# Split weights written to memory by the first batch and loaded finished by the other three

## The chip, the cores and the metric

The kernel runs on one core of a Trainium2 chip. The metric is device time in microseconds (us). The time before is 846.46 us, the median of three runs (843.69 to 851.68). The profiled execution is one more run of the same program, 848.2 us, with a span of 845.7 us from its first to its last instruction.

## The reference

Inputs arrive in float64, the attention's q, k and v in float32. B is 4, S is 448, the width is 768 (12 heads of 64). What is computed, for each batch:

```python
scores = q @ k.T / sqrt(64); mask above the diagonal; attn = softmax(scores)
x      = (attn @ v)                      # heads side by side: 448 x 768
gate   = sigmoid(causal_conv5(x, conv_w))
h      = gate * (x @ w_val)              # weight stage 0
x2     = h @ w_out                       # weight stage 1
theta  = x2 @ w_theta                    # weight stage 2
y      = w_tok_r @ (x2 * cos(theta)) + w_tok_i @ (x2 * sin(theta))
u      = x2 + y
out    = u + relu(u @ w_ch)              # weight stage 3
```

Four of the weights (w_val, w_out, w_theta, w_ch) are 768 x 768 and serve all four batches alike.

## The kernel before, in words

Every large matmul is made of three: a float32 operand x is split into a high part (rounded to the engine's fp32r format) and a low part (x minus high), and high*high, high*low and low*high are summed in PSUM. So each weight has to become a pair (high, low) in SBUF before TensorE (PE) can use it.

A weight stage has 6 column blocks of 128, and the four stages make 24 blocks, numbered n = 0 to 23 in batch 0, 24 to 47 in batch 1, and so on to 95 (`NW * B` = 96). A block is cut into two halves (g = 0, 1) of 384 rows; a half is a tile of 128 partitions x 384 elements. Half a block feeds 9 matmuls of 448 columns (`gemm`, L452).

A half goes through three steps:

- `load_w` (batch 0 only): a DMA of 384 KB brings the 64-bit words into a `cv_raw` buffer (3 KB a partition, 4 buffers).
- `stage_w`: in batch 0 `to_f32` turns the 64-bit words into float32 with three VectorE (DVE) operations (L152, L155, L159) and one of ScalarE (ACT, L158); the last one writes the `w_raw` tile (1.5 KB, 3 buffers), which a DMA (L210) also writes to a scratch tensor in memory. In the later batches a DMA (L212) loads `w_raw` from the scratch tensor.
- `split_w`: GpSimd (POOL) makes the high part (`pool_hi`, L104), and POOL (`pool_lo`, L107) or DVE (`dve_lo`, L110) the low part, into `w_hi` and `w_lo` (1.5 KB, 3 buffers each). It runs in all four batches. `W_DVE` says per batch and stage how many of the two halves' low parts go to DVE.

`gemm(n)` calls, for each half, `split_w` of block n+1, `stage_w` of block n+2 and `load_w` of block n+4, and then issues its 9 matmuls. The first two blocks (`AHEAD` = 2) are split into tiles of the activations' buffers and used by `gemm_ahead` while batch 0's attention runs.

Around it: all DMAs are issued from one queue, that of SyncE (SP), in order; an instruction on it that waits holds all behind it. Besides the weights these are q, k and v of the next heads, the results, and for each pair of heads the row sums' reciprocals, which go to memory (`rows<-rec`, L375) and come back spread over partitions (`rb<-rows`, L378). The dense stages of batch b run while the attention of batch b+1 is computed; the table `RATE` says how many attention steps stand between the dense steps. The framework's scheduler puts each engine's instructions in an order that is fixed before the run, and hands out the buffers of a tag.

Of the kernel before, what the change touches and what calls it, by code (L numbers as in the profile page):

```python
# [37 lines left out]
YLD = 1  # L38
ABS_DVE = (1, 0, 0, 0)
PIN = 2  # L40
W_DVE = ('0010', '1000', '0000', '2111')
TOK_AFTER = 5
LAG = 3
RATE = ((1.027, 1.063, 1.027), (1.029, 1.029, 1.089), (1.03, 1.03, 1.01), (1.057, 0.994, 1.041))
# [4 lines left out]
def kernel(  # L49
# [86 lines left out]
            )  # L136

    def setup_conv():
        t = pool.tile([P, CV, 2], I32, tag="cv_raw", name="cv_raw", bufs=4)
# [42 lines left out]
        dve_lo(wtok_l[:, m, :], pt[:, :S], wtok_h[:, m, :])  # L182

    stages = [w_val, w_out, w_theta, w_ch]
    scratch = dram.tile([NW, 2, P, KH * P], F32, name="scratch")
    bits = {}
    raws = {}
    splits = {}

    def load_w(n, g):  # L190
        if n < NW:
            e = n % KC
            t = pool.tile([P, CV, 2], I32, tag="cv_raw", name="cv_raw", bufs=4)
            nc.sync.dma_start(
                out=t.rearrange("p (c n) two -> p c (n two)", c=KH),
                in_=stages[n // KC][g * KH * P : (g + 1) * KH * P, 2 * e * P : 2 * (e + 1) * P].rearrange(
                    "(c p) n -> p c n", p=P
                ),
            )
            bits[n, g] = t  # L200

    def stage_w(n, g):
        if n >= NW * B:
            return
        t = pool.tile([P, KH, P], F32, tag="w_raw", name="w_raw", bufs=3)
        flat = t.rearrange("p c n -> p (c n)")
        if n < NW:
            to_f32(flat, bits.pop((n, g)))
            if B > 1:
                nc.sync.dma_start(out=scratch[n, g], in_=flat)  # L210
        else:
            nc.sync.dma_start(out=flat, in_=scratch[n % NW, g])  # L212
        raws[n, g] = t

    def split_w(n, g):
        if n >= NW * B:
            return
        t = raws.pop((n, g))
        if n < AHEAD:
            hi, lo = (  # L220
                pool.tile([P, S], F32R, tag=tag, name="w_ahead", bufs=12)[:, : KH * P].rearrange("p (c n) -> p c n", n=P)
                for tag in ("act_hi", "act_lo")
            )
        else:
            hi = pool.tile([P, KH, P], F32R, tag="w_hi", name="w_hi", bufs=3)
            lo = pool.tile([P, KH, P], F32R, tag="w_lo", name="w_lo", bufs=3)
# [213 lines left out]
    def gemm(acts):  # L440
        n = wn[0]
        wn[0] += 1
        pt = psum("mm")
        for g in range(2):
            split_w(n + 1, g)
            stage_w(n + 2, g)
            load_w(n + 4, g)
            whi, wlo = splits.pop((n, g))
            for kc in range(g * KH, (g + 1) * KH):
                xhi, xlo = acts[kc]  # L450
                for m, (a, x) in enumerate(((whi, xhi), (whi, xlo), (wlo, xhi))):
# [187 lines left out]
    for n in range(5 * (H + 1) + X_SEG + 1):  # L639
        next(at, None)  # L640
        if n == 5:
            setup_conv()
        for m in range(AHEAD):
            if n == W_AT + 4 * m:
                for g in range(2):
                    load_w(m, g)
            if n == W_AT + 4 * m + 2:
                for g in range(2):
                    stage_w(m, g)
                    split_w(m, g)  # L650
        i, c = divmod(n, 5)
        if AHEAD and i >= 4 and i % 2 == 0 and c == A_SEG and i // 2 - 2 < KC - 1:
            gemm_ahead(i // 2 - 2)
        if n == 5 * H - 5:
            for m in range(AHEAD, AHEAD + 2):
                for g in range(2):
                    load_w(m, g)
            for g in range(2):
                stage_w(AHEAD, g)
                load_w(AHEAD + 2, g)  # L660
        if n == 5 * H:
            for g in range(2):
# [52 lines left out]
```

## Time and profile before

| | before |
|---|---|
| median of three runs | 846.46 us (843.69 to 851.68) |
| profiled execution | 848.2 us, span 845.7 us |
| PE busy | 732.9 us (87%) |
| POOL busy | 515.9 us (61%) |
| DVE busy | 521.2 us (62%) |
| ACT busy | 414.1 us (49%) |
| mean granted clock of PE | 0.938 |
| moved by DMA | 88.28 MB |

The share of an engine is its busy time over the span. A granted clock of 1.00 is 2.4 GHz, of 0.5 is 1.2 GHz. The difference between the execution's time and its span, 2.5 us, lies outside the profile.

### The profile page before, as it was taken

The page shows a single profiled execution, that of the slowest core. Times are in us where ns is not written, and L with a number is a line of the kernel's source. Part 1 is how long each engine was busy: PE and PEld are TensorE (multiplying, and loading weights), DVE is VectorE, ACT ScalarE, POOL GpSimd, SP SyncE. Part 2 cuts the span into 40 slices and gives each one's busy share as a digit, 9 for nine tenths or more (in the row PEclk, how much of TensorE's full clock was granted, in tenths as well). Part 3 has the DMA queues.
Part 4 walks back from the last instruction along what each step waited for, and adds up shares of the span by engine and source line. Part 5 has one row for each costly group of instructions (what it writes and reads, how often), then busy time and mean ns, then how long its engine had stood idle before and what let it go on. Part 6 is the DMA issues. An engine that isn't in the chain of part 4 may idle for free.

```text
span 845.7 us, 12489 instructions
## 1 busy us (share of the span) xinstructions
PE 732.9 (87%) x3965; PEld 611.6 (72%) x3965; DVE 521.2 (62%) x1161; ACT 414.1 (49%) x982; POOL 515.9 (61%) x589
## 2 busy tenths in 40 slices
PE   6577589888397896999889898989989999999997
PEld 4446358666296785878768786868778787898996
DVE  6775698979878562744747644725637834436641
ACT  6667465545567642435558632525558621125311
POOL 3566559667434656577768745567848348676322
PEclk9879669999599898999989999999989999999999
DMA  9984743768534343444423224345332113433113
GB/s 223 185 146 85 139 89 106 206 174 176 181 91 107 61 119 102 82 125 100 101 57 82 52 69 108 89 118 98 84 92 49 32 49 103 132 112 84 36 31 102
DMA packets 151277, 88.28 MB, mean 104 GB/s; under 512 B 93455, under 2 KB 150317, under 8 KB 151213
## 3 DMA queue, kind: packets, MB, share of 16 engines
q1 hardware_dynamic: 151213, 87.51, 42.8%
q8 instruction: 31, 0.51, 0.3%
q14 instruction: 33, 0.27, 0.1%
HBM read 72.45 MB, written 15.03 MB: 103 GB/s over the span
## 4 chain that ended last, share of the span: by engine, by line
PE 47%; DMA 21%; DVE 18%; issue 4%; ACT 4%; POOL 3%; SPq 2%; ACTq 0%; POOLq 0%; DVEq 0%
PE ps_mm L452 23%; PE ps_mm L545 10%; DMA rows<-rec 7%; PE ps_av L357 4%; DMA w_raw<-scratch 4%; PE ps_tr L334 3%; DMA cv_raw<-in_moe_w_val_dram 3%; DMA cv_raw<-in_moe_w_ch_dram 2%; PE ps_s L313 2%; DMA cv_raw<-in_moe_w_theta_dram 2%; DVE w_raw L159 2%; DVE ps_s L315 2%; PE ps_s L314 2%; DVE gate L415 2%; PE ps_tr L531 1%
## 5 line engine op out<-in xcount | busy, mean ns | idle before, releaser
L104 POOL TENSOR_SCALAR w_hi<-w_raw 128x384 fp32r<-128x384 f32 x188 | 113.6, 605 | 151.1 <-PE ps_mm L452 90.1
L452 PE MATMUL ps_mm<-act_hi,w_lo 128*128 128x448 f32 x432 | 163.0, 378 | 8.3 <-POOL w_lo L107 6.4
L452 PE MATMUL ps_mm<-act_hi,w_hi 128*128 128x448 f32 x432 | 163.6, 381 | 6.5 <-POOL w_hi L104 2.1
L107 POOL TENSOR_TENSOR w_lo<-w_raw,w_hi 128x384 fp32r<-128x384 f32 x146 | 157.2, 1078 | 9.3
L452 PE MATMUL ps_mm<-act_lo,w_hi 128*128 128x448 f32 x432 | 159.9, 370 | 0.0
L115 ACT ACTIVATE prob<-ps_s,negm 112x112 f32<-112x112 f32 x192 | 95.2, 497 | 88.3 <-DVE negm L315 86.4
L315 DVE CUSTOM_DVE_ANT_0 ps_s<-ps_s,mask 112x112 f32<-112x112 f32 x192 | 85.6, 454 | 65.1 <-PE ps_s L314 54.4
L334 PE MATMUL ps_tr<-ident,prob 112*112 112x112 f32 x480 | 85.2, 280 | 19.0 <-ACT prob L115 13.1
L452 PEld LDWEIGHTS ps_mm<-act_hi,w_lo 128*128 128x128 f32 x432 | 82.9, 192 | 19.4 <-POOL w_lo L107 10.1
L452 PEld LDWEIGHTS ps_mm<-act_hi,w_hi 128*128 128x128 f32 x432 | 82.4, 192 | 16.0 <-POOL w_hi L104 4.0
L313 PE MATMUL ps_s<-kk,qs 128*112 128x256 f32 x192 | 74.0, 389 | 20.2 <-ACT prob L115 10.3
L452 PEld LDWEIGHTS ps_mm<-act_lo,w_hi 128*128 128x128 f32 x432 | 82.9, 192 | 5.5
L334 PEld LDWEIGHTS ps_tr<-ident,prob 112*112 112x112 f32 x480 | 59.3, 142 | 34.2 <-ACT prob L115 17.9
L107 POOL TENSOR_TENSOR act_lo<-x2f,act_hi 128x448 fp32r<-128x448 f32 x36 | 44.9, 1247 | 53.9 <-DVE act_hi L464 28.4
L347 ACT COPY pt<-ps_tr 112x448 f32<-112x448 f32 (+2 forms) x120 | 51.4, 441 | 48.3 <-PE ps_tr L334 47.6
L357 PE MATMUL ps_av<-pt,v_raw 112*64 112x336 f32 (+3 forms) x384 | 66.4, 451 | 1.7 <-ACT pt L347 1.3
L314 PE MATMUL ps_s<-klo,qs 128*112 128x256 f32 x192 | 62.8, 339 | 3.3 <-DVE klo L110 3.1
L545 PE MATMUL ps_mm<-wtok_h,zt_h 128*128 128x448 f32 x168 | 64.4, 383 | 0.5 <-ACT zt_h L536 0.4
L545 PE MATMUL ps_mm<-wtok_h,zt_l 128*128 128x448 f32 x168 | 63.6, 379 | 1.4 <-DVE zt_l L110 1.3
L545 PE MATMUL ps_mm<-wtok_l,zt_h 128*128 128x448 f32 x168 | 62.0, 369 | 0.0
L411 POOL TENSOR_TENSOR gate<-gate,tp 128x448 f32<-128x448 f32 x48 | 58.8, 1225 | 2.4
L313 PEld LDWEIGHTS ps_s<-kk,qs 128*112 128x112 f32 x192 | 36.7, 192 | 29.1 <-ACT prob L115 12.3
(101 smaller groups left out, 1518.3 us busy)
## 6 DMA issues: line engine op xcount, KB each, us to landing
w_raw<-scratch SPq DMA_DIRECT2D x144, 192.0 KB, 2.4
scratch<-w_raw SPq DMA_DIRECT2D x48, 192.0 KB, 2.8
q_raw<-in_q_dram SPq DMA_DIRECT2D x48, 112.0 KB, 3.0
k_raw<-in_k_dram SPq DMA_DIRECT2D x48, 112.0 KB, 3.3
v_raw<-in_v_dram SPq DMA_DIRECT2D x24, 224.0 KB, 3.2
rb<-rows SPq DMA_DIRECT2D x48, 112.0 KB, 3.3
out_dram<-o SPq DMA_DIRECT2D x24, 224.0 KB, 2.7
cv_raw<-in_moe_w_val_dram SPq DMA_DIRECT2D x12, 384.0 KB, 4.7
```

Of the source, the lines that this page charges most:

```text
L104: nc.gpsimd.tensor_scalar(out=dst, in0=src, scalar1=1.0, scalar2=0.0, op0=ALU.mult, op1=ALU.add)
L107: nc.gpsimd.tensor_tensor(out=dst, in0=src, in1=f32(hi), op=ALU.subtract)
L115: exps.append(nc.scalar.activation(*args, **kw))
L313: nc.tensor.matmul(pt[:CP, :nn], lhsT=qs[:, cs], rhs=kk[:, :nn], start=True, stop=False)
L314: nc.tensor.matmul(pt[:CP, :nn], lhsT=qs[:, cs], rhs=klo[:, :nn], start=False, stop=True)
L315: ttr = nc.vector.tensor_tensor_reduce(out=pt[:CP, :n], in0=pt[:CP, :n], in1=mask[:, S - n : S], scale=-1.0 / math.sqrt(D), scalar=3.0e38, ...
L334: nc.tensor.transpose(pt[:CP, off : off + CP], prob[i, c][:, kc * CP : (kc + 1) * CP], ident[:CP, :CP])
L347: nc.scalar.copy(t, src)
L357: nc.tensor.matmul(av[g][j * D : (j + 1) * D, kc * CP : S], lhsT=tv[:, j, kc, :], rhs=pT.pop((2 * g + j, kc)), start=kc == 0, stop=kc == N ...
L411: nc.gpsimd.tensor_tensor(out=gt, in0=gt, in1=tp, op=ALU.add)
L452: nc.tensor.matmul(pt[:, :S], lhsT=a[:, kc % KH, :], rhs=x, start=kc == 0 and m == 0, stop=kc == KC - 1 and m == 2,)
L545: nc.tensor.matmul(pt[:, :S], lhsT=a[:, m, :], rhs=w[:, m, :], start=m == 0 and n == 0, stop=m == NZ - 1 and n == 2,)
```

## The change

Only batch 0 stages and splits. `stage_w` writes the float32 words back into every second word of the `cv_raw` tile itself (so `w_raw` is gone), `split_w` reads them from there with a step of two words, and both parts go to memory: one DMA of 384 KB from the joint tile `w_hl` (high and low side by side, 3 KB), or for the first two blocks two DMAs of 192 KB. In the other three batches a new function, `fetch_w`, loads the finished pair with one DMA of 384 KB into a `w_hl` tile; `gemm(n)` calls it for block n+3. `load_w` moves from block n+4 to n+3. `cv_raw` and `w_hl` share one tag, `wb`, of 8 buffers of 3 KB, in place of the 4 buffers of 3 KB and 9 of 1.5 KB. `W_DVE` keeps its row for batch 0.

```diff
-W_DVE = ('0010', '1000', '0000', '2111')
+W_DVE = '0010'
...
-    scratch = dram.tile([NW, 2, P, KH * P], F32, name="scratch")
+    scratch = dram.tile([NW, 2, P, 2 * KH * P], F32, name="scratch")
...
     def load_w(n, g):
+        if n >= NW:
+            return
+        e = n % KC
+        t = pool.tile([P, CV, 2], I32, tag="wb", name="cv_raw", bufs=8)
...
     def stage_w(n, g):
         if n < NW:
-        t = pool.tile([P, KH, P], F32, tag="w_raw", name="w_raw", bufs=3)
-        flat = t.rearrange("p c n -> p (c n)")
-        if n < NW:
-            to_f32(flat, bits.pop((n, g)))
-            if B > 1:
-                nc.sync.dma_start(out=scratch[n, g], in_=flat)
-        else:
-            nc.sync.dma_start(out=flat, in_=scratch[n % NW, g])
-        raws[n, g] = t
+            to_f32(bits[n, g][:, :, 0], bits[n, g])
...
     def split_w(n, g):
-        if n >= NW * B:
-            return
-        t = raws.pop((n, g))
+        if n >= NW:
+            return
+        t = bits.pop((n, g))[:, :, 0].bitcast(F32).rearrange("p (c n) -> p c n", n=P)
...
-            hi = pool.tile([P, KH, P], F32R, tag="w_hi", name="w_hi", bufs=3)
-            lo = pool.tile([P, KH, P], F32R, tag="w_lo", name="w_lo", bufs=3)
+            hl = pool.tile([P, 2, KH, P], F32R, tag="wb", name="w_hl", bufs=8)
+            hi, lo = hl[:, 0], hl[:, 1]
         pool_hi(hi, t)
-        w = int(W_DVE[n // NW][n % NW // KC])
-        (dve_lo if w > g else pool_lo)(lo, t, hi)
+        (dve_lo if int(W_DVE[n // KC]) > g else pool_lo)(lo, t, hi)
+        if B > 1 and n < AHEAD:
+            for a, x in enumerate((hi, lo)):
+                nc.sync.dma_start(
+                    out=scratch[n, g][:, a * KH * P : (a + 1) * KH * P], in_=f32(x.rearrange("p c n -> p (c n)"))
+                )
+        elif B > 1:
+            nc.sync.dma_start(out=scratch[n, g], in_=f32(hl.rearrange("p a c n -> p (a c n)")))
         splits[n, g] = (hi, lo)
+
+    def fetch_w(n, g):
+        if not NW <= n < NW * B:
+            return
+        hl = pool.tile([P, 2, KH, P], F32R, tag="wb", name="w_hl", bufs=8)
+        nc.sync.dma_start(out=f32(hl.rearrange("p a c n -> p (a c n)")), in_=scratch[n % NW, g])
+        splits[n, g] = (hl[:, 0], hl[:, 1])
...
             split_w(n + 1, g)
             stage_w(n + 2, g)
-            load_w(n + 4, g)
+            load_w(n + 3, g)
+            fetch_w(n + 3, g)
```

The calls that fill the pipeline in batch 0's attention move by one block too: `load_w(AHEAD + 2)` goes from the step with `n == 5 * H - 5` to the one with `n == 5 * H`, where `load_w(AHEAD + 3)` stood.

## Rows read from the trace of the kernel before

**Rows 1.** Busy time by stretch: us, PE, PEld, DVE, ACT, POOL, clock, DMA, GB/s.
```profile
133.00:211.00 78.00, 67.07 (x353) 54.84 (x352) 69.42 (x135) 38.04 (x94) 57.40 (x60) 0.98 0.65 174
...
342.00:531.00 189.00, 175.05 (x985) 147.61 (x985) 106.47 (x246) 94.67 (x225) 130.21 (x147) 0.97 0.37 88
531.00:717.00 186.00, 172.93 (x963) 145.77 (x962) 104.14 (x240) 92.62 (x212) 120.51 (x138) 0.97 0.31 77
717.00:846.00 129.00, 121.50 (x627) 110.88 (x625) 60.44 (x98) 34.93 (x65) 62.01 (x79) 0.99 0.30 84
```

**Rows 2.** Tile w_raw from 342 to 846 us: users (ns min/median/max), waits.
```profile
L104 POOL TENSOR_SCALAR w_hi<-w_raw x141: 505/513/1331, 343.8 to 833.9; 128x384 fp32r<-128x384 f32 x141
...
L107 POOL TENSOR_TENSOR w_lo<-w_raw,w_hi x107: 992/1016/1525, 344.4 to 834.5; 128x384 fp32r<-128x384 f32 x107
...
  DMA w_raw<-scratch: 35.0, 10
...
  PEld ps_mm L452: 19.2, 15
  PE ps_mm L452: 12.8, 8
```

**Rows 3.** Chain that ended last, from 603 us: start, us, what.
```profile
603.47 7.15 DMA rows<-rec
...
612.58 2.90 DMA w_raw<-scratch
...
616.10 1.01 POOL w_lo L107
...
617.16 5.46 PE ps_mm L452 x16
```

**Rows 4.** Busy time by stretch around that wait, columns as in rows 1.
```profile
614.50:621.50 7.00, 4.34 (x12) 3.87 (x13) 1.14 (x3) 2.47 (x4) 5.44 (x7) 0.51 0.42 122
```

**Rows 5.** Whom PE waited for, 342 to 846 us: us, times, longest.
```profile
PE ps_tr L531 <- DVE z L520: 5.1, 4, 1.7
PE ps_tr L572 <- ACT o L576: 3.7, 1, 3.7
PE ps_tr L531 <- POOL z L521: 1.9, 1, 1.9
...
PE ps_s L313 <- POOL kk L104: 1.0, 1, 1.0
```

**Rows 6.** Groups of instructions by line, whole span: busy us, mean ns.
```profile
L159 DVE SCALAR_TENSOR_TENSOR w_raw<-cv_raw 128x384 int32<-128x384 int32 x48 | 32.5, 677 | 5.1 <-POOL w_lo L107 5.0
...
L155 DVE SCALAR_TENSOR_TENSOR cv_raw<-cv_raw 128x384 int32<-128x384 int32 x48 | 31.7, 663 | 0.4
```

**Rows 7.** DMA queue (packets, MB, share of 16 engines) and issues (count, KB, us).
```profile
q1 hardware_dynamic: 151213, 87.51, 42.8%
...
w_raw<-scratch SPq DMA_DIRECT2D x144, 192.0 KB, 2.4
...
cv_raw<-in_moe_w_theta_dram SPq DMA_DIRECT2D x12, 384.0 KB, 4.3
...
rows<-rec SPq DMA_DIRECT2D x24, 3.5 KB, 7.2
```

**Rows 8.** Matmuls of line 452 alone in one stretch, columns as in rows 1.
```profile
133.00:211.00 78.00, 53.45 (x226) 41.65 (x227) 0.98 0.65 174
```

**Rows 9.** Timeline of DVE: start, us, instruction; one half being staged.
```profile
185.86 0.35 DVE L152 TENSOR_SCALAR cv_raw<-cv_raw 128x384 int32<-128x384 uint32 x1
...
188.74 1.52 DVE L159 SCALAR_TENSOR_TENSOR w_raw<-cv_raw 128x384 int32<-128x384 int32 x1
```

**Rows 10.** What the SP queue waited for, whole span: us, times, longest.
```profile
SPq L378 <- DMA rows<-rec: 153.5, 24, 8.5
```

**Rows 11.** The chain's shares of the span by line, from the page.
```profile
PE ps_mm L452 23%; PE ps_mm L545 10%; DMA rows<-rec 7%; PE ps_av L357 4%; DMA w_raw<-scratch 4%; PE ps_tr L334 3%; DMA cv_raw<-in_moe_w_val_dram 3%; DMA cv_raw<-in_moe_w_ch_dram 2%; PE ps_s L313 2%; DMA cv_raw<-in_moe_w_theta_dram 2%; DVE w_raw L159 2%; DVE ps_s L315 2%; PE ps_s L314 2%; DVE gate L415 2%; PE ps_tr L531 1%
```

**Rows 12.** Groups of instructions by line, 342 to 846 us: busy us, mean ns.
```profile
L520 DVE TENSOR_TENSOR z<-z,x2f 128x448 f32<-128x448 f32 x18 | 17.6, 980 | 15.4 <-ACT z L519 15.4
...
L521 DVE TENSOR_TENSOR z<-z,x2f 128x448 f32<-128x448 f32 x6 | 3.7, 623 | 6.1 <-ACT z L518 6.1
```

More of the change, by code (lines that the diff above doesn't have):

```diff
@@ L138, in setup_conv @@
     def setup_conv():
-        t = pool.tile([P, CV, 2], I32, tag="cv_raw", name="cv_raw", bufs=4)
+        t = pool.tile([P, CV, 2], I32, tag="wb", name="cv_raw", bufs=8)
         nc.sync.dma_start(
@@ L184, with stage_w, split_w @@
     stages = [w_val, w_out, w_theta, w_ch]
-    scratch = dram.tile([NW, 2, P, KH * P], F32, name="scratch")
+    scratch = dram.tile([NW, 2, P, 2 * KH * P], F32, name="scratch")
     bits = {}
-    raws = {}
     splits = {}
     def load_w(n, g):
-        if n < NW:
[L192 to L202, printed above, removed]
-        if n >= NW * B:
-            return
-        t = pool.tile([P, KH, P], F32, tag="w_raw", name="w_raw", bufs=3)
-        flat = t.rearrange("p c n -> p (c n)")
-        if n < NW:
-            to_f32(flat, bits.pop((n, g)))
-            if B > 1:
-                nc.sync.dma_start(out=scratch[n, g], in_=flat)
-        else:
-            nc.sync.dma_start(out=flat, in_=scratch[n % NW, g])
-        raws[n, g] = t
-    def split_w(n, g):
-        if n >= NW * B:
-            return
-        t = raws.pop((n, g))
+        if n >= NW:
+            return
+        e = n % KC
+        t = pool.tile([P, CV, 2], I32, tag="wb", name="cv_raw", bufs=8)
+        nc.sync.dma_start(
+            out=t.rearrange("p (c n) two -> p c (n two)", c=KH),
+            in_=stages[n // KC][g * KH * P : (g + 1) * KH * P, 2 * e * P : 2 * (e + 1) * P].rearrange(
+                "(c p) n -> p c n", p=P
+            ),
+        )
+        bits[n, g] = t
+    def stage_w(n, g):
+        if n < NW:
+            to_f32(bits[n, g][:, :, 0], bits[n, g])
+    def split_w(n, g):
+        if n >= NW:
+            return
+        t = bits.pop((n, g))[:, :, 0].bitcast(F32).rearrange("p (c n) -> p c n", n=P)
         if n < AHEAD:
@@ L224, in split_w @@
         else:
-            hi = pool.tile([P, KH, P], F32R, tag="w_hi", name="w_hi", bufs=3)
-            lo = pool.tile([P, KH, P], F32R, tag="w_lo", name="w_lo", bufs=3)
+            hl = pool.tile([P, 2, KH, P], F32R, tag="wb", name="w_hl", bufs=8)
+            hi, lo = hl[:, 0], hl[:, 1]
         pool_hi(hi, t)
-        w = int(W_DVE[n // NW][n % NW // KC])
-        (dve_lo if w > g else pool_lo)(lo, t, hi)
-        splits[n, g] = (hi, lo)
+        (dve_lo if int(W_DVE[n // KC]) > g else pool_lo)(lo, t, hi)
+        if B > 1 and n < AHEAD:
+            for a, x in enumerate((hi, lo)):
+                nc.sync.dma_start(
+                    out=scratch[n, g][:, a * KH * P : (a + 1) * KH * P], in_=f32(x.rearrange("p c n -> p (c n)"))
+                )
+        elif B > 1:
+            nc.sync.dma_start(out=scratch[n, g], in_=f32(hl.rearrange("p a c n -> p (a c n)")))
+        splits[n, g] = (hi, lo)
+    def fetch_w(n, g):
[4 more added lines that the diff above has]
+        splits[n, g] = (hl[:, 0], hl[:, 1])
     v_ins = {}
@@ L659 @@
                 stage_w(AHEAD, g)
-                load_w(AHEAD + 2, g)
         if n == 5 * H:
@@ L664 @@
                 stage_w(AHEAD + 1, g)
-                load_w(AHEAD + 3, g)
+                load_w(AHEAD + 2, g)
     if AHEAD:
```

## The prediction

> **What bounds the kernel now.** I read the busy time by stretch first. It is cut at 133, 342, 531 and 717 us, where the first weight matmuls of batches 0 to 3 run. From 342 us on PE is busy 175.05 + 172.93 + 121.50 = 469.5 of 504 us, so 34.5 us stand open, 27 of them in batches 1 and 2; no other engine is above 70% there. In batch 0's first weight stages (133 to 211 us) it is different: DVE, which converts the weights, is busy 69.42 of 78 us and DMA has 0.65 of its capacity in use [rows 1].
>
> Then I read the tile that the change removes. From 342 us on, PE waited 12.8 us in 8 waits for what is made from `w_raw`, and the weight loads on PE 19.2 us; POOL itself stood 35.0 us before tiles that a DMA had not yet brought [rows 2]. The chain shows how one such wait arises: a transfer of row sums takes 7.15 us, SP stands behind it, the load of `w_raw` is issued only at 612.58 and lands 2.9 us later, POOL makes the two parts, and sixteen matmuls then take 5.46 us [rows 3]. In the 7 us around this wait the granted clock was 0.51, so PE, idle for a part of them, ran near 1.2 GHz [rows 4]. What else PE waited for after 342 us are ends of chains on DVE, ACT and POOL [rows 5].
>
> **The change part by part.** *Splits removed.* In batches 1 to 3 all 141 high parts and 107 low parts go from POOL, 141 x 0.513 + 107 x 1.016 = 181 us by the medians [rows 2], and the low parts on DVE with them. POOL is not the bound there (at most 130.21 of 189 us [rows 1]), so the busy time by itself brings nothing. What counts is what waited for it: the 12.8 us of PE [rows 2]. To that comes the slow clock after these waits. There are three such stretches, of which one stands; in it PE was busy 4.34 us at half clock [rows 4], which is about 2.2 us of lost time, and two more of about 3.5 us cost 1.7 us each. With 5.6 us of clock the waits are worth 18.4 us. POOL's other products come sooner too: PE waited 1.9 + 1.0 us for them [rows 5]. Gross gain 21.3 us.
>
> What is late next? The waits for DVE's and ACT's products, 5.1 and 3.7 us at the largest [rows 5], stay, and PE will reach some of them earlier and stand there longer. The bounds of what is kept are nothing and all of 21.3; I take three quarters, 16 us, because those two are together 8.8 us, less than the weights' own 12.8.
>
> *Loads moved and doubled.* A fetch waits only for a buffer that an earlier block's matmuls have left: 8 halves are 4 blocks, so it is asked for some three blocks before its use, where today POOL has to work between the landing and the use. From 342 to 531 us 24 blocks run, 7.9 us each [rows 1], so SP may stand 6.4 us behind row sums (153.5 us in 24 waits [rows 10]) without PE seeing it. Bytes: 144 loads grow by 192 KB and 48 stores too, 37.7 MB more. The queue moved 87.51 MB in 42.8% of the sixteen engines' time [rows 7], so its share would grow to about 61%: bandwidth is there, and I cost it at nothing on PE while the three blocks of lead hide it; without that lead a fetch costs its 4.3 us, the time of a load of the same size [rows 7].
>
> *Conversion in place.* The last DVE operation now writes with a step of two words. L155 does that already and takes 663 ns, L159 writes densely and takes 677 [rows 6]: nothing. No row shows POOL reading with a step of two; by DVE's rows that is free as well, and at worst it doubles the high parts of batch 0, 48 x 0.5 = 24 us of an engine that has 78 - 57.4 us idle in the tightest stretch [rows 1]. I take nothing.
>
> *Buffers of batch 0.* This is the part that costs. Today the buffer of a load is free when the conversion is done, since `w_raw` takes over. After the change a load for block n+3 follows the split of block n+1 in the program and waits until POOL has made its low part. So four halves share one round: landing 4.3 us [rows 7], conversion from 185.86 to 190.26, 4.4 us [rows 9], split 1.5 us [rows 2], together 10.2 us, or 2.6 us for a half. The stretch from 133 to 211 us shows 226 matmuls of L452 [rows 8], nine to a half, so 25 halves at 3.1 us each. The round still fits, with 4 x 3.1 - 10.2 = 2.2 us to spare, where today's round of 8.7 us (no split in it) has 3.7. The bounds are nothing (DVE sets the pace of this stretch) and 30 us (the third rival). I take 3 us, nearer to nothing, because the average round fits. Stores of 384 KB come after the split instead of 192 KB after the conversion; SP stands at them a little longer, and queued behind it are the next load, q, k and v and the row sums; that is within the 3 us.
>
> *Sum.* 848.2 - 16 + 3 = 835.2 us for the profiled execution. That one lies 1.7 us above the median of the runs, so 833.5, rounded to 834.
>
> **The rivals.** *More than that.* All 21.3 us are kept, batch 0 loses nothing, and DVE gets faster too: the product z takes 980 ns on DVE at L520, and 623 ns in the same shape at L521, which DVE runs in the batch where POOL does not make a z beside it [rows 12]. If all 18 of L520 after 342 us gained the difference, that is 6.4 us on a chain that PE waits for [rows 5]. 848.2 - 21.3 - 6.4 - 1.7 = 819. Against it: the chains of attention and of the dense part are interleaved in a fixed order, so a gain of POOL seldom comes through whole. The Trainium skill ("SBUF — State Buffer", Who interferes with whom) says that a DVE instruction with two SBUF inputs contends with a GpSimd instruction that reads SBUF; by that rule the 980 and the 623 ns are the same work with and without POOL beside it, and the gain would be this rival's. The two rows agree with the rule but do not prove it.
>
> *The gain is given back at the row sums.* Chain and queue say that row sums matter: `rows<-rec` has 7% of the chain [rows 11], about 59 us, though it carries 3.5 KB and takes 7.2 us [rows 7]. If a fetch of double size stands before it, it lands later by what the fetch takes longer than today's: 4.3 less 2.4 us [rows 7] is 1.9 at most, and nothing where no fetch stands before it; I take two thirds, 1.3. For the 12 row sums of batches 1 and 2, all on the chain, that is 15.6 us: 848.2 - 16 + 3 + 15.6 - 1.7 = 849. Against it: part of the 7% is there only because SP, standing behind row sums, issued a weight late [rows 3], and that link is cut. By the Trainium skill ("DMA: Bandwidth & Descriptors", Queues, rings and completion order) each DMA engine consumes the descriptors of one queue in ring order; as all DMAs here come from SP, by that rule row sums do stand behind a fetch issued earlier, which is this rival's mechanism. No row before shows its price.
>
> *Slower: the weights of batch 0 become the bound.* The round of four halves decides. Beyond 12.4 us (10.2 + 2.2) each further microsecond is lost on the stage. A wait of SP behind row sums, 6.4 us on average [rows 10], makes a round of 16.6, 4.2 us too long, and POOL can be held by other work before the split on top; I put 5 us on each. Batch 0's dense part sees 6 of the 24 row sums: 30 us. 848.2 - 16 + 30 - 1.7 = 860.5, about 861. For it: DVE is busy 89% of the stretch [rows 1] and an engine that waits in order for a late load cannot catch up. Against it: the pipeline starts filled by eight halves.
>
> **How the numbers follow.** The forecast (834, its own range 826 to 842) has 0.42; more than that (819) 0.16; given back (849) 0.20; slower (861) 0.22. A measurement of this kernel can tell a change from none at about 1%, so faster means below 838 and slower above 855. Of the forecast's 0.42 I put 0.32 below 838 and 0.10 above. Faster: 0.32 + 0.16 = 0.48. Same: 0.10 + 0.20 = 0.30. Slower: 0.22. The range of 818 to 858 leaves out about half of the fastest case below and about half of the slow one above, 0.08 + 0.10; it takes in all bounds but the full loss in batch 0.
>
> **What would show it.** Right: after batch 0 no wait of PE for a weight is longer than a few tenths, POOL's busy time falls by about 180 us, the stretches of batches 1 and 2 (189 and 186 us) shorten by some 7 us each, and the granted clock there is nearer to 1.00. DMA's share rises to about 60%. The stretch from 133 to 342 us, 209 us today, stays within 5 us. The forecast falls if DVE stands before L152 for much longer than now or if that stretch grows by over 10 us (the slow rival); if `rows<-rec` takes over 8.5 us at the median and keeps its 7% of the chain (given back); or if PE waits in batches 1 and 2 for the fetched tile itself, which would mean that the buffers do not run ahead.

## The result and the profile after

| | before | after |
|---|---|---|
| median of the runs | 845.51 us (4 runs) | 820.75 us (4 runs, 819.74 to 821.24) |
| ratio | | 0.9693 (95% interval 0.9642 to 0.9744) |
| profiled execution, span | 845.7 us | 818.0 us |
| PE busy | 732.9 us (87%) | 729.8 us (89%) |
| POOL busy | 515.9 us (61%) | 316.5 us (39%) |
| DVE busy | 521.2 us (62%) | 489.7 us (60%) |

The forecast was 834 us, 12 us faster than before; it became 25 us faster. The changed kernel was timed twice more, on other chips: 0.9635 [0.9581, 0.9690] and 0.9656 [0.9591, 0.9721].

To see where the time came from I cut the span where the first weight matmul of block 2 (end of batch 0's first attention), of block 24 (batch 1) and of block 72 (batch 3) starts. The table holds every kernel of this study; a length is that of one profiled execution, and the changed kernel's three executions show how far such a length scatters. In e2, e4, e6 and e11 PE's order mixes the first matmuls of block 24 with the last of block 23; the cut stands in every kernel where the 397th weight matmul after the first cut starts (22 blocks of 18 are 396), which in these four is 1.8 us behind the first matmul of block 24.

| kernel | to block 2 | 2 to 24 | 24 to 72 | 72 to end | median of runs |
|---|---|---|---|---|---|
| before | 133.0 | 208.9 | 374.5 | 129.3 | see each group |
| after | 129.4 | 198.2 | 361.1 | 129.3 | 820.75 |
| after, again (e10, e15) | 130.3, 131.8 | 198.4, 197.1 | 357.1, 361.6 | 129.5, 129.7 | 818.86, 820.56 |
| e1: parts made again | 129.7 | 197.6 | 367.3 | 134.1 | 828.49 |
| e2: old buffers, n+4 | 136.7 | 204.5 | 351.4 | 129.3 | 828.47 |
| e11: old buffers, n+3 | 139.5 | 205.0 | 351.6 | 129.4 | 827.71 |
| e12: eight buffers, n+4 | 131.5 | 217.0 | 352.8 | 129.3 | 830.93 |
| e4: six buffers | 124.6 | 223.4 | 357.7 | 129.3 | 834.42 |
| e3: fetched twice | 132.3 | 194.0 | 402.1 | 136.5 | 869.36 |
| e7: half the bytes | 130.7 | 195.2 | 357.1 | 129.4 | 813.49 |
| e5: no stores | 130.8 | 193.8 | 357.8 | 130.9 | 814.83 |
| e6: dead work | 126.8 | 218.0 | 360.7 | 129.3 | 838.13 |
| e8: loads of block 5 held | 128.9 | 197.4 | 359.6 | 129.3 | 820.13 |
| e9: early loads spread | 130.6 | 195.0 | 362.1 | 129.5 | 817.59 |
| e13: low parts to POOL | 130.2 | 203.9 | 358.5 | 129.3 | 823.98 |
| e14: lighter DVE | 129.4 | 196.7 | 355.9 | 129.4 | 818.50 |

The 27.7 us between the two spans are 3.6 before block 2, 10.7 in the rest of batch 0 and 13.4 in batches 1 and 2; batch 3 gave nothing. About half came from batch 0, for which the forecast had a loss. The kernel before has one profile only. From block 2 to 24 the changed kernel's three profiles lie within 1.3 us, but e1, e3 and e7, which change nothing in batch 0 except the first work for batch 1, took 197.6, 194.0 and 195.2 us: differences of 4 us in that column are not clear of the scatter.

Here is the busy time by stretch, columns as in [rows 1]; first of the kernel before, cut at its blocks 2, 24 and 72:

```profile
133.00:341.90 208.90, 170.54 (x918) 140.52 (x917) 152.78 (x323) 108.49 (x251) 126.74 (x135) 0.92 0.51 133
341.90:716.40 374.50, 347.49 (x1944) 293.06 (x1942) 210.12 (x484) 187.08 (x435) 250.11 (x284) 0.97 0.34 82
```

and of the changed kernel:

```profile
129.40:327.60 198.20, 169.91 (x919) 138.24 (x917) 157.53 (x323) 107.38 (x252) 120.59 (x129) 0.96 0.70 188
327.60:688.70 361.10, 342.87 (x1943) 295.14 (x1942) 195.77 (x478) 195.58 (x442) 103.04 (x102) 0.97 0.55 142
688.70:818.00 129.30, 122.09 (x631) 111.59 (x629) 41.80 (x70) 34.15 (x64) 14.24 (x13) 1.00 0.49 144
```

In batches 1 and 2 PE's open time fell from 374.5 - 347.5 = 27.0 to 18.2 us, while POOL's work more than halved. The other 4.6 of the 13.4 us are PE's busy time, 347.5 before and 342.9 after (338.7 in e10, 344.0 in e15); the matmuls are as many, and why they were busy for less was not found. In batch 0 PE's work is the same (170.5 and 169.9 us), and what fell is its open time, from 38.4 to 28.3 us. DVE did more in a shorter time: its open time there fell from 56.1 to 40.7 us.

Whom PE waited for in batches 1 and 2, first in the kernel before (us, times, longest; [rows 5] and PE's waits in [rows 2] reach to the end of batch 3):

```profile
PE ps_mm L452 <- POOL w_lo L107: 6.0, 3, 4.6
PE ps_mm L452 <- POOL w_hi L104: 5.8, 3, 2.6
...
PE ps_tr L531 <- DVE z L520: 3.0, 2, 1.7
```

and in the changed kernel:

```profile
PE ps_tr L536 <- DVE z L525: 3.6, 4, 1.4
PE ps_mm L550 <- ACT zt_h L541: 2.8, 3, 2.3
PE ps_av L361 <- ACT o L581: 2.8, 1, 2.8
PE ps_tr L338 <- ACT prob L115: 2.7, 2, 2.1
PE ps_av L361 <- ACT pt L351: 2.4, 1, 2.4
...
PE ps_mm L457 <- POOL x_lo L107: 0.5, 1, 0.5
```

No wait for a weight is left. The ends of DVE's and ACT's chains are what stands there now. Added up over this stretch, 12.5 us of waits for weights are gone, and those for POOL's other products went from 2.9 to 0.5; but the waits for ACT grew from 5.9 to 11.9 us and those for DVE's other products from 5.1 to 5.5. Some 6 of 15 us were taken up by what is late next.

DMA issues of the changed kernel (counterpart of [rows 7]):

```profile
q1 hardware_dynamic: 151789, 125.25, 59.9%
...
w_hl<-scratch SPq DMA_DIRECT2D x144, 384.0 KB, 3.9
scratch<-w_hl SPq DMA_DIRECT2D x44, 384.0 KB, 3.7
...
rows<-rec SPq DMA_DIRECT2D x24, 3.5 KB, 7.6
```

The queue's share is 59.9%, and the row sums take 7.6 us, 0.4 more than before. On the chain that ended last, by line, their share went from 7% [rows 11] to 3%:

```profile
PE ps_mm L457 26%; PE ps_mm L550 9%; DMA out_dram<-o 3%; DMA rows<-rec 3%; PE ps_av L361 3%; PE ps_tr L338 2%; DMA cv_raw<-in_moe_w_ch_dram 2%; DVE gate L419 2%; PE ps_s L317 1%; DVE qs L110 1%; PE ps_s L318 1%; PE ps_tr L536 1%; ACT prob L115 1%; DMA cv_raw<-in_moe_w_theta_dram 1%; ACT L523 1%
```

### The profile page after: what moved, and what is told of

The parts are those of the page before. It is cut to its first block, busy times and chain, and to the rows that moved or that the text cites. A ratio compares the mean times of both kernels' runs of the same rounds, so it can differ in the third digit from the quotient of the medians.

```text
span 818.0 us, 11973 instructions
## 1 busy us (share of the span) xinstructions
PE 729.8 (89%) x3965; PEld 613.4 (75%) x3965; DVE 489.7 (60%) x1125; ACT 420.6 (51%) x988; POOL 316.5 (39%) x337
## 3 DMA queue, kind: packets, MB, share of 16 engines
q1 hardware_dynamic: 151789, 125.25, 59.9%
## 4 chain that ended last, share of the span: by engine, by line
PE 45%; DVE 11%; DMA 10%; ACT 7%; issue 2%; POOL 1%; SPq 1%; ACTq 0%; POOLq 0%; DVEq 0%
PE ps_mm L457 26%; PE ps_mm L550 9%; DMA out_dram<-o 3%; DMA rows<-rec 3%; PE ps_av L361 3%; PE ps_tr L338 2%; DMA cv_raw<-in_moe_w_ch_dram 2%; DVE gate L419 2%; PE ps_s L317 1%; DVE qs L110 1%; PE ps_s L318 1%; PE ps_tr L536 1%; ACT prob L115 1%; DMA cv_raw<-in_moe_w_theta_dram 1%; ACT L523 1%
## 5 line engine op out<-in xcount | busy, mean ns | idle before, releaser
L457 PE MATMUL ps_mm<-act_hi,w_hl 128*128 128x448 f32 x864 | 273.8, 378 | 6.1 <-POOL w_hl L104 2.4
L457 PEld LDWEIGHTS ps_mm<-act_hi,w_hl 128*128 128x128 f32 x864 | 165.0, 192 | 23.1 <-POOL w_hl L104 3.5
L457 PE MATMUL ps_mm<-act_lo,w_hl 128*128 128x448 f32 x432 | 161.6, 375 | 0.3 <-DVE act_lo L110 0.3
L457 PEld LDWEIGHTS ps_mm<-act_lo,w_hl 128*128 128x128 f32 x432 | 82.9, 192 | 6.3 <-DVE act_lo L110 0.5
L338 PEld LDWEIGHTS ps_tr<-ident,prob 112*112 112x112 f32 x480 | 59.9, 143 | 32.1 <-ACT prob L115 19.6
L457 PE MATMUL ps_mm<-x_hi,w_hl 128*128 128x448 f32 x264 | 79.4, 369 | 0.6 <-DVE hf L494 0.5
L361 PE MATMUL ps_av<-pt,v_raw 112*64 112x224 f32 (+3 forms) x384 | 65.3, 453 | 6.2 <-ACT o L581 2.8
L361 PEld LDWEIGHTS ps_av<-pt,v_raw 112*64 112x64 f32 x384 | 29.8, 150 | 42.3 <-issue 21.6
L107 POOL TENSOR_TENSOR x_lo<-xf,x_hi 128x448 fp32r<-128x448 f32 x23 | 28.3, 1231 | 75.1 <-ACT x_hi L398 74.6
L526 POOL TENSOR_TENSOR z<-z,x2f 128x448 f32<-128x448 f32 x18 | 21.6, 1197 | 85.8 <-ACT z L523 85.8
```

The lines of the kernel that those rows point to most:

```text
L107: nc.gpsimd.tensor_tensor(out=dst, in0=src, in1=f32(hi), op=ALU.subtract)
L338: nc.tensor.transpose(pt[:CP, off : off + CP], prob[i, c][:, kc * CP : (kc + 1) * CP], ident[:CP, :CP])
L361: nc.tensor.matmul(av[g][j * D : (j + 1) * D, kc * CP : S], lhsT=tv[:, j, kc, :], rhs=pT.pop((2 * g + j, kc)), start=kc == 0, stop=kc == N ...
L457: nc.tensor.matmul(pt[:, :S], lhsT=a[:, kc % KH, :], rhs=x, start=kc == 0 and m == 0, stop=kc == KC - 1 and m == 2,)
L526: (nc.vector if Z_DVE[b] else nc.gpsimd).tensor_tensor(out=t, in0=t, in1=x2f[e], op=ALU.mult)
```

## The experiments

**First group: each half of the change alone, more bytes, fewer buffers** (the kernel before took 849.61 us on this chip, median of 7 runs).

*e1* keeps batch 0 as changed, but later batches make both parts again from what they fetched.

```diff
         if n >= NW:
-            return
+            fh, fl = splits.pop((n, g))
+            hl = pool.tile([P, 2, KH, P], F32R, tag="wb", name="w_hl", bufs=8)
+            hi, lo = hl[:, 0], hl[:, 1]
+            pool_hi(hi, f32(fh))
+            z = zero.rearrange("p (c n) -> p c n", n=P)
+            (dve_lo if int(W_DVE[n // NW][n % NW // KC]) > g else pool_lo)(lo, f32(fl), z)
+            splits[n, g] = (hi, lo)
```

> Batches 1 to 3 fetch the finished pair as the changed kernel does and then make both parts once more, on POOL and DVE with the old table, into a second buffer of the same set; the result is the same. Batch 0 is that of the changed kernel. If the splits on the way to PE are what cost batches 1 and 2 their time, their stretch from block 24 to block 72 grows from 361 us back towards 374 (13 us), and the total is near 834 us, with batch 0 still 14 us shorter than before (block 24 starts near 328 us). If that gain came from the order of the instructions or from the loads alone, the total stays at 821 to 824 us.

828.49 us, ratio 0.9754 [0.9715, 0.9792]. Its stretches from block 24 on:

```profile
327.30:694.60 367.30, 345.48 (x1943) 294.15 (x1942) 209.99 (x480) 192.98 (x442) 247.77 (x284) 0.96 0.59 138
694.60:828.70 134.10, 125.01 (x631) 113.67 (x629) 70.67 (x101) 36.05 (x67) 66.03 (x79) 0.97 0.49 146
```

POOL carries 247.8 us again, as much as before the change, and 24 to 72 takes 367.3 us: 5.7 to 10.2 us more than the three executions of the changed kernel, yet 7 less than before. Batch 3 loses 5 us, which it did not gain by the change; this kernel holds a second buffer for each half, so that cost need not be the splits alone. Batch 0 ends where it does in the changed kernel (327.3 us). The removed splits are thus worth some 8 us of the whole (5 to 10 by the ratios), and batch 0's gain does not come from them.

*e2* keeps the finished loads and gives batch 0 its old buffers and its old distance of loads.

```diff
-        t = pool.tile([P, CV, 2], I32, tag="wb", name="cv_raw", bufs=8)
+        t = pool.tile([P, CV, 2], I32, tag="cv_raw", name="cv_raw", bufs=4)
...
-            to_f32(bits[n, g][:, :, 0], bits[n, g])
+            t = pool.tile([P, KH, P], F32, tag="w_raw", name="w_raw", bufs=3)
...
-            hl = pool.tile([P, 2, KH, P], F32R, tag="wb", name="w_hl", bufs=8)
+            hl = pool.tile([P, 2, KH, P], F32R, tag="w_hl", name="w_hl", bufs=3)
...
-            load_w(n + 3, g)
+            load_w(n + 4, g)
```

> Finished loads as in the changed kernel, but batch 0 keeps the buffers of the kernel before: 4 of 3 KB for the loaded words, 3 of 1.5 KB for the converted ones, 3 of 3 KB for the pairs, loads for block n+4; batches 1 to 3 fetch into 7 of these. Theory A, the one set of buffers with conversion in place gave batch 0 its 14 us: block 24 starts at 338 to 343 us as before, total 831 to 835 us. Theory B, batch 0 gained by the pair's stores and the early fetches for batch 1: block 24 starts near 328 us, total 819 to 823 us.

828.47 us, ratio 0.9761 [0.9723, 0.9800]. The cut at block 24 stands at 341.2 us (its first matmul at 339.3), about where it stood before the change (341.9). Whom PE waited for in batch 0:

```profile
PE ps_mm L460 <- POOL w_hl L104: 8.4, 2, 6.4
PE ps_mm L460 <- DVE w_hl L110: 5.2, 3, 4.4
```

and whom POOL waited for there:

```profile
POOL w_hl L104 <- PE ps_mm L460: 13.7, 11, 4.9
POOL w_hl L104 <- DMA scratch<-w_hl: 13.2, 6, 6.5
```

With three buffers for the pair, POOL stands until a pair is used (13.7 us) and until its store has landed (13.2 us). So batch 0's gain hangs on the buffers. The second wait is new: before the change no pair was stored, so e2 is not the old batch 0 with one thing altered. The whole kernel loses only 8 us by it, not 14, since 24 to 72 is 6 to 10 us shorter here:

```profile
341.20:692.60 351.40, 335.19 (x1943) 289.51 (x1941) 195.76 (x476) 194.49 (x439) 102.30 (x101) 1.00 0.56 140
```

The granted clock of that stretch is 1.00 in place of 0.97 (3.4 us at half clock; 20.5, 10.2 and 23.4 in the changed kernel's three executions), and PE is busy 335.2 us in place of 342.9. Why the clock stayed up was not tried.

Either half alone brings 21 of the 849.6 us. The whole brings 26 to 31 by its three ratios, so the two overlap.

*e3* fetches each finished half twice.

```diff
-        nc.sync.dma_start(out=f32(hl.rearrange("p a c n -> p (a c n)")), in_=scratch[n % NW, g])
+        for _ in range(2):
+            nc.sync.dma_start(out=f32(hl.rearrange("p a c n -> p (a c n)")), in_=scratch[n % NW, g])
```

> The changed kernel, but each finished half is fetched twice into the same tile, so 56 MB more are moved. If fetches in front of the row sums cost time (the rival 'given back'), the row sums take longer than 7.6 us and each of the 12 in batches 1 and 2 costs another 1.3 us or more: 836 us or above. If the three blocks of lead hide the fetches, 820 to 824 us.

869.36 us, ratio 1.0236 [1.0195, 1.0276]. Its stretch from 24 to 72, two of its DMA issues, and PE's largest wait in that stretch:

```profile
326.30:728.40 402.10, 354.04 (x1946) 300.62 (x1944) 195.55 (x478) 187.04 (x439) 103.03 (x102) 0.94 0.86 226
```

```profile
w_hl<-scratch SPq DMA_DIRECT2D x288, 384.0 KB, 6.5
...
rows<-rec SPq DMA_DIRECT2D x24, 3.5 KB, 9.2
```

```profile
PE ps_mm L458 <- DMA w_hl<-scratch: 30.5, 15, 9.3
```

and what SP waited for longest there:

```profile
SPq L234 <- DMA w_hl<-scratch: 103.5, 71, 4.9
```

At a DMA share of 0.86 the lead of three blocks no longer hides a fetch. But the edit does two things: more bytes move, and, as both fetches of a half go into one tile, SP stands 103.5 us until a fetch has landed, which it never does in batches 1 and 2 of the changed kernel. Which of the two costs the 41 us was not separated. In the changed kernel, at a share of 0.55, no matmul waits for a fetch.

*e4* has six shared buffers in place of eight (`bufs=6`).

> The changed kernel with 6 buffers of 3 KB in place of 8. If the run-ahead is what batch 0 gained by, or what hides the row sums' waits in batches 1 and 2, the time goes up by 6 to 15 us, to 827 to 836 us, and waits of PE for the pair appear. If it is only the missing splits, it stays at 820 to 823 us.

834.42 us, ratio 0.9822 [0.9768, 0.9877]. PE's waits for weights in batch 0:

```profile
PE ps_mm L457 <- POOL w_hl L107: 11.1, 7, 3.4
...
PE ps_mm L457 <- POOL w_hl L104: 5.0, 4, 3.6
```

Two buffers less cost 25 us from block 2 to 24. Of these, 14.6 are PE's open time (its waits for POOL's parts went from 3.6 to 16.1 us) and 10.6 its busy time, 180.5 in place of 169.9 us, at a granted clock of 0.91 in place of 0.96. A loss of this kind is what the forecast saw for the changed kernel; it is real, with six.

**Second group: bytes, POOL's load, early loads** (before: 847.77 us).

*e7* fetches 192 KB for each half; it uses the high part in place of the low one too.

```diff
-        nc.sync.dma_start(out=f32(hl.rearrange("p a c n -> p (a c n)")), in_=scratch[n % NW, g])
-        splits[n, g] = (hl[:, 0], hl[:, 1])
+        nc.sync.dma_start(out=f32(hl[:, 0].rearrange("p c n -> p (c n)")), in_=scratch[n % NW, g][:, : KH * P])
+        splits[n, g] = (hl[:, 0], hl[:, 0])
```

> The changed kernel, but batches 1 to 3 fetch only the high part of each half (192 KB in place of 384 KB) and use it in place of the low part as well (so the low parts are left out of the result of these batches; the matmuls are as many). Theory (the doubled bytes are hidden behind three blocks of lead): within 1% of the changed kernel, 817 to 823 us, batches 1 and 2 from block 24 to 72 at 358 to 362 us. Rival (the doubled fetch holds up the row sums): rows<-rec goes from 7.6 back to 7.2 us or less, and some 0.4 us on each of 18 row sums come back, 813 us. Rival (bytes cost by the rate of the kernel that fetched each half twice, 56.6 MB for 48 us): 28 MB less give 24 us, 797.

813.49 us, ratio 0.9607 [0.9564, 0.9649], 0.3 to 0.9% below the changed kernel's three ratios, whose intervals it overlaps. Of its DMA issues:

```profile
rows<-rec SPq DMA_DIRECT2D x24, 3.5 KB, 7.2
```

The row sums are back at 7.2 us and the time is the 813 us that the second theory said, but its 24 to 72 (357.1 us) is within the 357.1 to 361.6 of the changed kernel, so that theory is neither shown nor ruled out. The doubled bytes cost between nothing and 7 us; the 24 us of e3's slope they do not cost.

*e6* adds the old splits as work that nobody waits for.

```diff
         if n >= NW:
-            return
+            d = dummy.rearrange("p (c n) -> p c n", n=P)
+            pool_hi(d, f32(dsrc))
+            (dve_lo if int(W_OLD[n // NW - 1][n % NW // KC]) > g else pool_lo)(d, f32(dsrc), dsrc)
```

> The changed kernel with the old work of POOL and DVE added as dead work: in batches 1 to 3 the same high and low parts are computed from a fixed tile into a tile that nobody reads. The parts that PE uses are the fetched ones. Theory (what batches 1 and 2 gained is that PE no longer waits for POOL's parts): 820 to 823 us, no more than the changed kernel. Rival (POOL's occupation itself costs: its other products come later, and DVE's z of L525 takes longer beside it): as the kernel that made the parts again, 826 to 830, with the mean of DVE z at that line back near 980 ns.

838.13 us, ratio 0.9896 [0.9848, 0.9945], slower than either theory had it, but not where they looked. Its stretches:

```profile
126.80:344.80 218.00, 177.78 (x919) 146.36 (x918) 180.28 (x331) 110.73 (x253) 182.12 (x206) 0.90 0.62 169
344.80:705.50 360.70, 339.47 (x1942) 290.94 (x1941) 218.30 (x506) 193.80 (x441) 222.44 (x277) 0.98 0.56 142
705.50:834.80 129.30, 122.09 (x631) 111.58 (x628) 42.72 (x70) 34.41 (x65) 14.99 (x13) 1.00 0.49 147
```

From block 24 on nothing is lost, with 222 us of POOL work in place of 103 (250 before the change): POOL's occupation is free there up to that amount, and what the splits cost was the wait. The planned order had put a third of the dead work into batch 0, and that stretch took 20 us longer; 7.9 of them are PE's busy time, at a granted clock of 0.90 in place of 0.96. The groups by line of POOL and of DVE in batch 0 show what stood there (busy us, mean ns | idle before); first one of the dead groups on POOL:

```profile
L108 POOL TENSOR_TENSOR dummy<-wtok_h 128x384 f32<-128x384 f32 x35 | 35.0, 999 | 0.3
```

and two groups of DVE that are not dead:

```profile
L153 DVE TENSOR_SCALAR cv_raw<-cv_raw 128x384 int32<-128x384 uint32 x36 | 26.4, 733 | 5.9 <-DMA cv_raw<-in_moe_w_ch_dram 3.1 <-DMA cv_raw<-in_moe_w_theta_dram 1.4 <-DMA cv_raw<-in_moe_w_out_dram 1.2
...
L111 DVE TENSOR_TENSOR w_hl<-cv_raw,w_hl 128x384 fp32r<-128x384 f32 x6 | 5.9, 988 | 0.0
```

The same two lines of the changed kernel, same stretch (busy us, mean ns):

```profile
L152 DVE TENSOR_SCALAR cv_raw<-cv_raw 128x384 int32<-128x384 uint32 x36 | 19.4, 538 | 10.8 <-DMA cv_raw<-in_moe_w_ch_dram 5.4 <-DMA cv_raw<-in_moe_w_out_dram 2.6 <-POOL w_hl L107 2.3
...
L110 DVE TENSOR_TENSOR w_hl<-cv_raw,w_hl 128x384 fp32r<-128x384 f32 x6 | 3.3, 550 | 0.0
```

DVE's own instructions became longer beside a busy POOL: its busy time in batch 0 went from 157.5 to 180.3 us, of which only some 5 us are dead work.

*e8* issues the loads of block 5 behind the v of the eighth pair of heads, the second of batch 1 (its expectation says the seventh); *e9* those of blocks 4 and 5 behind the v of the fourth and fifth pair (`HOLD` is {5: 7} and {4: 3, 5: 4}; `load_now` is the old `load_w`).

```diff
     def load_w(n, g):
+        if n in HOLD:
+            with tc.issue_after(v_ins[HOLD[n]].ins):
+                load_now(n, g)
+        else:
+            load_now(n, g)
```

> The changed kernel, but the loads of block 5 (both halves) are issued after the v of the seventh pair of heads, at about 119 us in place of 39 and 43, so that these two halves are converted after 120 us and not during batch 0's attention. The eight buffers stay. Theory (batch 0's gain is a head start of DVE: two more halves are converted before block 2, where before the three buffers of w_raw forbade it): the stretch from block 2 to block 15 grows by DVE's work for two halves, 2 x 2.2 us and its waits, from 92.7 to 97 or 98; total 825. Rival (the gain is made in each round, since a buffer is free more often): that stretch stays within 2 us of 92.7; total 819 to 822.

820.13 us, ratio 0.9695 [0.9641, 0.9748]; from block 2 to 15 it took 90.9 us where the changed kernel takes 92.7. The loads went out at 114.1 and 117.0 us, and the conversions of the two halves ended at 126.5 and 129.4 us, with block 2 at 128.9. So the head start was hardly taken away, and the run decides nothing about it.

> The changed kernel, but the loads of block 4 are issued after the v of the fourth pair of heads (42 us in place of 27 and 38) and those of block 5 after the v of the fifth (58 in place of 40 and 43), out of the stretch from 25 to 50 us in which the DMA share is 1.06. Theory (the early loads hold up q, k and v of the first attention steps: with six buffers, that is two loads less, block 2 began 5 us earlier): block 2 at 125 and not 129.4, the rest as it was, 816 to 818 us in total. Rival (the first attention is paced by its own chains): block 2 at 129, total 819 to 822.

817.59 us, ratio 0.9649 [0.9605, 0.9693]; block 2 at 130.6 us. The loads went out at 45.1 us (block 4) and at 64.4 and 68.8 us (block 5), and block 2 began no earlier: nothing shows the early loads holding up the first attention. No difference can be told.

**Third group: buffers against distance** (before: 852.12 us; the changed kernel, *e10*, stood beside the others).

> The changed kernel itself, unaltered, so that the others of this group stand beside it on one chip: 819 to 823 us, ratio 0.966 to 0.972.

818.86 us, ratio 0.9635 [0.9581, 0.9690].

*e11* is e2 with `load_w(n + 3, g)`.

> The kernel with the old buffers of batch 0 and finished loads afterwards, but with batch 0's loads called for block n+3 as in the changed kernel (in the earlier run they were called for n+4 as before). Theory (distance: with n+3 fewer conversions stand ahead of the z products in DVE's fixed order, 19 in place of 24 from block 2 to the first z of L525): from block 2 to block 24 197 to 201 us, as in the changed kernel, total 818 to 822. Rival (buffers: the conversion in place frees DVE from the three buffers of w_raw): 203 to 208 us from block 2 to 24, as with the old buffers and n+4 (204.4), total 826 to 830.

827.71 us, ratio 0.9746 [0.9681, 0.9811]. From block 2 to 24 it takes 205.0 us against 204.5 with n+4: with the old buffers the distance makes no difference.

*e12* is the changed kernel with `load_w(n + 4, g)`.

> The changed kernel with its eight buffers, but batch 0's loads called for block n+4 in place of n+3. Theory (distance): the order of DVE and SP goes back to more conversions ahead, from block 2 to 24 205 to 209 us, total 828 to 832. Rival (buffers): 196 to 200 us, total 818 to 822.

830.93 us, ratio 0.9782 [0.9721, 0.9842], and 217.0 us from block 2 to 24, worse than either theory's figure. PE's waits for weights there:

```profile
PE ps_mm L457 <- POOL w_hl L107: 7.7, 7, 2.9
PE ps_mm L457 <- POOL w_hl L104: 6.5, 2, 5.1
```

One block further, the loads seem to take the buffers that POOL needs for the next pair: POOL stood 20.8 us for the matmuls of an older pair, 14.9 in the changed kernel. Of the 18.8 us that this stretch is longer than in the changed kernel, 6.5 are PE's open time and 12.3 its busy time, at a granted clock of 0.88 in place of 0.96. So neither buffers nor distance makes the gain alone: eight shared buffers do, with loads three blocks ahead. More lead or fewer buffers cost 19 to 25 us against that from block 2 to 24.

*e5* leaves out the stores of 22 blocks.

```diff
-        elif B > 1:
+        elif False:
             nc.sync.dma_start(out=scratch[n, g], in_=f32(hl.rearrange("p a c n -> p (a c n)")))
...
-        nc.sync.dma_start(out=f32(hl.rearrange("p a c n -> p (a c n)")), in_=scratch[n % NW, g])
+        nc.sync.dma_start(out=f32(hl.rearrange("p a c n -> p (a c n)")), in_=scratch[n % AHEAD, g])
```

> The changed kernel, but batch 0 writes only its first two blocks to memory, and the later batches fetch these two over and over (so 22 of the 24 blocks' stores are left out, and the later batches compute with wrong weights; the fetches are as many and as large). Theory (the stores hide behind SP's other waits): batch 0 as in the changed kernel, block 24 at 326 to 329 us, total 819 to 823. Rival (the stores of 384 KB take bandwidth from the loads, DMA share 0.85 there, and SP stands 57 us before them): block 2 to 24 five to ten us shorter, 811 to 816.

814.83 us, ratio 0.9577 [0.9517, 0.9637], against 0.9635 of the changed kernel beside it. From block 2 to 24 it takes 193.8 us, 3 to 5 us less; but e3, with all its stores, took 194.0. The intervals overlap too: a cost of the stores is not shown.

**Fourth group: what sets the pace in batch 0** (before: 847.49 us).

*e13* sets `W_DVE = '0000'`; *e14* also `H_LO = (0, 0, 1, 0)`, which gives the low parts of h in batch 0 to POOL; *e15* is the changed kernel.

> The changed kernel, but the six low parts of the third weight stage that DVE makes in batch 0 go to POOL as the others do (3.3 us of DVE work less from block 2 to 24, about 6.7 us of POOL work more). Theory (DVE's queue sets the pace of batch 0, and what stands on it ahead of the first z counts): the stretch from block 2 to 15 gets 2 to 4 us shorter than 92.5, total 815 to 818. Rival (what counts is when a buffer comes free, that is POOL's split): PE waits longer for w_hl of POOL, the stretch grows by 2 to 5 us, total 821 to 825.

823.98 us, ratio 0.9703 [0.9647, 0.9759]; 203.9 us from block 2 to 24.

> As the one before, and the six low parts of h in batch 0 (5.1 us on DVE) go to POOL too. Theory (DVE sets the pace): from block 2 to 24 up to 8 us shorter than 198.3, total 811 to 816. Rival (POOL's splits hold the buffers, and POOL then carries 13 us more): 200 to 206 us from block 2 to 24, total 822 to 828.

818.50 us, ratio 0.9636 [0.9578, 0.9693]; 196.7 us from block 2 to 24, columns as in [rows 1]:

```profile
129.40:326.10 196.70, 172.89 (x919) 140.94 (x916) 158.34 (x311) 110.70 (x253) 137.61 (x140) 0.95 0.67 189
```

> The changed kernel itself once more, beside the two: 817 to 822 us, ratio 0.963 to 0.970, from block 2 to 24 198 to 199 us.

820.56 us, ratio 0.9656 [0.9591, 0.9721]; 197.1 us.

Both theories fall as single causes. Taking 3.3 us from DVE made batch 0 some 6 us longer, though PE's waits for POOL's parts did not grow (3.0 us, 3.6 in the changed kernel), and taking 5.1 more from it, with POOL at 137.6 us, made it as short as in the changed kernel. DVE's busy time did not even fall (158.3 us): its instructions lengthen beside POOL, and each edit also gives another planned order. Changes of 5 us in batch 0 can't be put down to one engine's load.

## Why the prediction was right and wrong

**Splits removed: right in size, wrong in one part.** The term was 16 us; between block 24 and 72 the profiled pair shows 13.4, with the two other executions 17.4 and 12.9. The 12.8 us of PE's waits for weights are gone, and the chains said to be late next are: PE's waits for ACT took up 6 us, so that its open time fell by 8.8. The rest of the 13.4 is busy time, whose cause stays open. But the clock did not come back: the time at half clock in this stretch was 20.5 us before and 20.5, 10.2 and 23.4 us in three executions after. I had counted 5.6 us for it.

**Loads doubled, at nothing: close.** e7 bounds it at 0 to 7 us, and e5, 4 us faster than the changed kernel beside it, shows no clear cost of the stores. Row sums took 0.4 us longer, where the rival that gives the gain back reckoned with 1.3 each. Its mechanism shows up: 7.2 us with 192 KB, 7.6 with 384, 9.2 with twice 384. SP still stood 74.0 us behind them in batches 1 and 2 (76.9 before), but no matmul waited for a weight by it, and their share of the chain halved.

**Conversion in place, at nothing: right.** Groups by line in batch 0, before and after (busy us, mean ns | idle before):

```profile
L107 POOL TENSOR_TENSOR w_lo<-w_raw,w_hi 128x384 fp32r<-128x384 f32 x36 | 40.8, 1132 | 2.3
L104 POOL TENSOR_SCALAR w_hi<-w_raw 128x384 fp32r<-128x384 f32 x44 | 29.0, 660 | 30.1 <-PE ps_mm L452 15.8 <-DVE w_raw L159 11.5 <-DMA cv_raw<-in_moe_w_theta_dram 2.5
...
L152 DVE TENSOR_SCALAR cv_raw<-cv_raw 128x384 int32<-128x384 uint32 x34 | 18.4, 543 | 17.8 <-DMA cv_raw<-in_moe_w_ch_dram 8.4 <-DMA cv_raw<-in_moe_w_out_dram 6.4 <-DMA cv_raw<-in_moe_w_theta_dram 3.0
```

```profile
L107 POOL TENSOR_TENSOR w_hl<-cv_raw,w_hl 128x384 fp32r<-128x384 f32 x34 | 38.2, 1124 | 2.1
...
L104 POOL TENSOR_SCALAR w_hl<-cv_raw 128x384 fp32r<-128x384 f32 x40 | 26.2, 654 | 40.1 <-PE ps_mm L457 14.9 <-DVE cv_raw L159 12.4 <-ACT pt L351 2.5
```

POOL reads with a step of two words in 654 and 1124 ns, densely in 660 and 1132. DVE's last operation, L159, now writes with that step: where POOL was idle beside it, it took 553 ns at the median, and 550 densely before. Its mean went up from 682 to 755 ns, all of it where POOL was at work beside it.

**Buffers of batch 0: the step that failed.** It was put at +3 us with bounds of 0 and 30; measured are -10.7 us from block 2 to 24 and -3.6 before it (in e10 and e15 -10.5 and -11.8, and -2.7 and -1.2). What the runs showed in its place is a gain with eight shared buffers and loads three blocks ahead, and the loss that the term had in mind only with six buffers (e4) or loads four blocks ahead (e12). The working compared the time of a round with the pace of the stretch, found both to fit, and so could only find a loss. Two readings were missing. First, PE's waits were read from 342 us on; in batch 0 they were larger. These are PE's before the change:

```profile
PE ps_tr L531 <- DVE z L520: 15.5, 2, 13.2
...
PE ps_tr L572 <- DVE x2f L583: 5.4, 1, 5.4
```

and after, where x2f no longer stands among the larger ones:

```profile
PE ps_tr L536 <- DVE z L525: 5.8, 1, 5.8
```

PE waited for products that stand behind the conversions on DVE. Second, DVE was called busy, but it also waited: L152, shown above, stood 17.8 us for loads before the change and 10.8 after, 8.4 of them for loads, and L159 stood 5.0 us until POOL's split freed a `w_raw`, which is in [rows 6] itself and was passed over. In the trace, L159 ended the conversion of 24 halves between block 2 and the first z of L520, and of 19 after the change; L152 began 22 in both, and two more halves were done before block 2 (12 against 10). That the buffers make the gain is shown by e2, e11, e4 and e12; how it passes through DVE's order and its loads is read from the traces, not shown: e8, e13 and e14 did not separate it.

**The slow rival** was no fancy: in e4 and e12 PE waits for POOL's parts as it said (16.1 and 14.2 us). It had no term for the clock, and PE's longer busy time is 10.6 and 12.3 us of what they lose. With eight buffers the limit lay elsewhere. One half of block 8 was loaded at 143.1 us, its low part was done at 155.4 and the next load went out at 155.8, a round of 12.7 us, just beyond the 12.4 reckoned; the 0.3 us over would be too little to see.

**More than that (819)** has nearly the measured time, for another reason: DVE's z at L525 takes 960 ns on average from 342 us on, not 623; batch 0 brought what it did not. That its z would get faster does not follow from its own rows: 623 ns were measured where POOL makes no z beside it, and the change leaves POOL's z (L526) where it was. Of the 18, 11 ran beside that z and took 1.10 to 1.49 us, and the 7 others 0.62.

## What to carry to other kernels

When a change gives buffers another shape, read who waits for a buffer in every stage, also in the one that is thought to pay; a stage with an engine at 89% can still have that engine waiting for loads and buffers. A pool shared by two uses needs the right lead for its room: here eight buffers and three blocks gain 11 us from block 2 to 24, and six buffers or four blocks lose 8 to 15 against before (more buffers or less lead were not tried). Moving work off an engine that is not the bound was worth the waits on it, less what was late next, and the doubled bytes were nearly free as long as the lead covered the landing: try it at twice the load, into a tile of its own, so that the test adds no wait.

## What the runs showed of the hardware

*DVE's instructions depend on what POOL does beside them.* In batch 0 of the changed kernel L152, with one input, took 356 ns at the median where POOL was idle (10 instructions) and 575 where POOL was busy for over half of it (23); in e6 353 (3) and 702 ns (30). L155, with two inputs, took 544 (3 instructions) and 876 ns (32) in e6. For example, at 308.81 us in the changed kernel an L152 met a low part that POOL had begun 375 ns before; it took 1180 ns and ended 222 ns after POOL. The Trainium skill ("SBUF — State Buffer", Who interferes with whom) says that a DVE instruction with two SBUF inputs contends with a GpSimd instruction that reads SBUF, and that `tensor_scalar` can enter a mode that does when its operands allow it; the traces agree with both. With it go the 20 us that e6 lost in batch 0, where DVE's busy time grew by 23 us; that the one made the other is not shown. The z of L525 shows it most plainly: from 342 us on it took 624 ns at the median where POOL was idle (6 instructions) and 1118 where POOL was busy for over half of it (12), and before the change L520 took 619 (3) and 1119 (15).

*The clock falls at the same places, but not in each execution.* In the changed kernel stretches at half clock begin 10 to 13, 87 to 89, 176 to 178, 268 to 270 and 353 to 359 us after block 24 in two of three executions; the third shows only the first, second and last. The stretch then took 357.1 in place of 361.1 and 361.6 us, and PE was busy 338.7 us in place of 342.9 and 344.0. A difference of 4 us between two single profiles of this kernel says nothing by itself.
